# Queueing the early loads in the order of need and starting attention from q and k

## The chip, the cores and the metric

One core of one Trainium2 chip. Times are device microseconds of that core: each kernel is executed several times, and the median is quoted. Profiles are of one execution, whose span is some 2 us shorter than the quoted time. A run is called slow when it is over 1.5% above the fastest of its kernel; only fast runs are compared. Ratios below are the mean time of one kernel's fast runs over that of the other's of the same rounds on the same chip, so not quite the ratio of the medians quoted beside them.

## The reference, cut to what matters

```python
x: (1, 2048, 1024) bf16            # S = 2048, D = 1024, 32 heads of 32
# block A: pre-LN, local dilated attention: 8 keys per position, 2 apart
q, k, v = layernorm(x) @ wqkv
logits  = einsum(q, k[pos - 2*w]) * 32**-0.5     # w = 0..7, masked at the start
h       = x + (softmax(logits) @ v[...]) @ wo
# block B: pre-LN, bilinear GLU, F = 3584
h2      = h + ((layernorm(h) @ w_gate) * (layernorm(h) @ w_up)) @ w_down
```

## The kernel before

The sequence is cut into four chunks of 512 positions. TensorE runs the qkv projections of all chunks, then per chunk the output projection and the GLU. VectorE runs the local attention of each chunk beside that, on data that goes through DRAM to change its layout: the projection is evicted by ScalarE, stored (`qd`, `kd`, `vd`), loaded again (`qD`, `kD`, `vD`), and the attention output goes the same way back (`od`, `oT`). The attention and the layer norms of chunks 1 to 3 are Python generators. A counter (`bg.now`) advances by 1.73 for each group of eight matmuls emitted, and decides where in the program order the generators' instructions are put. Each engine executes its own instructions in that order (in the profile after, for one, ScalarE stands 21.58 us before one activation, and the evictions placed behind it wait as well).

The early part of it:

```python
    load_x0(0)                  # four row tiles of chunk 0, and
    load_x0(1)
    load_w(2)                   # ... projection block 0 (1 MB, two halves)
    load_x0(2)
    load_w(2)                   # ... projection block 1
    load_x0(3)
    ...
    def first_transpose(t):     # chunk 0: transposed by TensorE
        pts[t] = psum.tile([128, KO, 128], BF, tag="mm", name=f"pt{t}")
        for kk in range(KO):
            nc.tensor.transpose(pts[t][:, kk, :], lns[t][:, bass.ts(kk, 128)], ident[:])
        nc.scalar.copy(lnTs[0][:, 0:4, bass.ts(t, 128)], pts[t][:, 0:4, :])
    def first_copy(t):
        nc.vector.tensor_copy(lnTs[0][:, 4:8, bass.ts(t, 128)], pts[t][:, 4:8, :])
    ...
    nc.gpsimd.tensor_copy(order_after_x0[:], x0[3][:, 0:1])
    pump()                      # SyncE: blocks 2 to 5 and half of wo
    bg.add(ln1(1))              # these load their own rows, on GpSimd's queue;
    bg.add(ln1(2))              # each norm is followed by its DMA transpose on SyncE
```

and the order of the main part:

```python
    def start_attention(c):
        stored.add(c)
        atts[c] = attention(c)          # for c == 0: load q, k, v, then 7.0 later
        bg.add(atts[c], bg.now + (5.0 if c == 0 else 0.0))

    qkv(0, range(1, 6))
    bg.add(ln1(3))
    start_attention(0)
    qkv(1, range(6))
    start_attention(1)
    qkv(2, range(6))
    start_attention(2)
    ...
    qkv(3, range(4), last=True)
    bg.finish(atts[0])
    nxt = wo_ln2(0)                     # needs oT of chunk 0; VectorE adds and normalises
    qkv(3, range(4, 6), last=True)
    start_attention(3)
    for c in range(NCH):                # GLU, then the next chunk's output projection
        ...
```

Of the kernel before, what the change touches and what calls it, by code (L numbers as in the profile page):

```python
# [8 lines left out]
BF = mybir.dt.bfloat16  # L9
# [66 lines left out]
def kernel(  # L76
# [62 lines left out]
        for b in range(4):  # L139
            stream.append((("wd", NCH - 1, hf, b), wd_v[:, bass.ts(b, 7), bass.ts(hf, 512)], 7))  # L140
    wts = {}
    state = {"next": 0, "live": 0}

    def pump(eng=None):
        while state["next"] < len(stream) and state["live"] < 7:
            key, src, n = stream[state["next"]]
            wt = wpool.tile([128, KO, 512], BF, tag="w", name="w_" + "_".join(map(str, key)))
            (eng or nc.sync).dma_start(wt[:, 0:n, :], src)
            wts[key] = wt
            state["next"] += 1  # L150
            state["live"] += 1

# [20 lines left out]
    def ln_tiles(name):  # L173
        mv4 = small.tile([128, 4, nc.vector.BN_AGGR_DIM], F32, tag="mv4", name="mv" + name)
        rs4 = small.tile([128, 4], F32, tag="rs4", name="rs" + name)
        return mv4, rs4

    def load_x(c, what, eng):
        tiles = []
        for t in range(4):  # L180
            xt = hp.tile([128, D], BF, tag="h", name=f"{what}{c}_{t}")
            eng.dma_start(xt[:], x[bass.ds(c * TC + t * 128, 128), :])
            tiles.append(xt)
        return tiles

    lnTs = {}

    def ln1(c):
        xts = load_x(c, "x", nc.gpsimd)
        yield "later", 8.0 if c < 3 else 5.0  # L190
        lnTs[c] = lnTp.tile([128, KO, TC], BF, tag="lnT", name=f"lnT1_{c}")
        mv4, rs4 = ln_tiles(f"1_{c}")

        def norm(t):
            ln = normalize(xts[t], mv4, rs4, t)
            nc.sync.dma_start_transpose(lnTs[c][:, :, bass.ts(t, 128)], ln[:])

        for t in range(4):
            stats(xts[t], mv4, t)
            rstd_of(mv4, rs4, t, t + 1)  # L200
            yield 1.5
            if t > 0:
                norm(t - 1)
                yield 0.55
        norm(3)
        yield 0.55


    def load_w(parts=1):
        key, src, n = stream[state["next"]]  # L210
        wt = wpool.tile([128, KO, 512], BF, tag="w", name="w_" + "_".join(map(str, key)))
        for q in range(parts):
            nc.sync.dma_start(wt[:, bass.ts(q, KO // parts), :], src[:, bass.ts(q, KO // parts), :])  # L213
        wts[key] = wt
        state["next"] += 1
        state["live"] += 1

    x0 = [hp.tile([128, D], BF, tag="h", name=f"x0_{t}") for t in range(4)]

    def load_x0(t):  # L220
        nc.sync.dma_start(x0[t][:], x[bass.ds(t * 128, 128), :])  # L221

    load_x0(0)
    load_x0(1)
    load_w(2)
    load_x0(2)
    load_w(2)
    load_x0(3)
    nc.scalar.preload_act_table_set("natural_log_exp_and_others")
    warm = const.tile([128, 512], BF)  # L230
# [52 lines left out]
        lns[t] = normalize(x0[t], mv0, rs0, t)  # L283

    def first_transpose(t):
        pts[t] = psum.tile([128, KO, 128], BF, tag="mm", name=f"pt{t}")
        for kk in range(KO):
            nc.tensor.transpose(pts[t][:, kk, :], lns[t][:, bass.ts(kk, 128)], ident[:])  # L288
        nc.scalar.copy(lnTs[0][:, 0:4, bass.ts(t, 128)], pts[t][:, 0:4, :])  # L289

    def first_copy(t):
        nc.vector.tensor_copy(lnTs[0][:, 4:8, bass.ts(t, 128)], pts[t][:, 4:8, :])  # L292

    def first_mm(t, kos):
        for ko in kos:
# [20 lines left out]
        if t < 3:  # L316
            first_rstd(t + 1)
    first_mm(3, range(8))
    order_after_x0 = const.tile([128, 1], BF)
    nc.gpsimd.tensor_copy(order_after_x0[:], x0[3][:, 0:1])  # L320
    pump()
    bg.add(ln1(1))
    bg.add(ln1(2))
    for j in range(4):
# [35 lines left out]
    def prefetch_qk(c):  # L360
        if c in stored and ("q", c) not in qkv_in:
            load_qk(c)

    def attention(c):
        if c == 0:
            load_qk(0)
            load_v(0)
            yield "later", 7.0
        qD, kD, vD = qkv_in["q", c], qkv_in["k", c], qkv_in["v", c]
        lg = att.tile([128, W, SUB], F32, tag="lg", name=f"lg{c}")  # L370
        for wp in range(W // 2):
            prod = att.tile([128, 2, DH, SUB], BF, tag="prod", name=f"prod{c}_{wp}")
            for j in range(2):
                o = HB - DIL * (2 * wp + j)
                nc.vector.tensor_tensor(prod[:, j], qD[:], kD[:, :, o:o + SUB], ALU.mult)  # L375
                yield 2.3
            nc.vector.tensor_tensor(prod[:, :, 0:16], prod[:, :, 0:16], prod[:, :, 16:32], ALU.add)  # L377
            yield 2.3
            nc.vector.tensor_tensor(prod[:, :, 0:8], prod[:, :, 0:8], prod[:, :, 8:16], ALU.add)
            yield 1.2  # L380
            t3 = att.tile([128, 2, 4, SUB], F32, tag="t3", name=f"t3{c}_{wp}")
            nc.vector.tensor_tensor(t3[:], prod[:, :, 0:4], prod[:, :, 4:8], ALU.add)
            yield 1.2
            nc.vector.tensor_tensor(t3[:, :, 0:2], t3[:, :, 0:2], t3[:, :, 2:4], ALU.add)
            nc.vector.tensor_tensor(lg[:, 2 * wp:2 * wp + 2, :], t3[:, :, 0], t3[:, :, 1], ALU.add)
            yield 1.0
        if c == 0:
            nc.vector.tensor_tensor(lg[0:32, :, 0:16], lg[0:32, :, 0:16], mask[:], ALU.add)
        tr = att.tile([128, 4, SUB], F32, tag="t3", name=f"tr{c}")
        nc.vector.tensor_tensor(tr[:], lg[:, 0:4], lg[:, 4:8], ALU.max)  # L390
        nc.vector.tensor_tensor(tr[:, 0:2], tr[:, 0:2], tr[:, 2:4], ALU.max)
        mx = att.tile([128, SUB], F32, tag="mx", name=f"mx{c}")
        nc.vector.tensor_tensor(mx[:], tr[:, 0], tr[:, 1], ALU.max)
        nc.vector.tensor_tensor(lg[:], lg[:], mx[:, None, :].to_broadcast((128, W, SUB)), ALU.subtract)
        nc.scalar.activation(lg[:], lg[:], ACTF.Exp, scale=float(DH) ** -0.5)
        yield 3.5
        tr2 = att.tile([128, 4, SUB], F32, tag="t3", name=f"trs{c}")
        nc.vector.tensor_tensor(tr2[:], lg[:, 0:4], lg[:, 4:8], ALU.add)
        nc.vector.tensor_tensor(tr2[:, 0:2], tr2[:, 0:2], tr2[:, 2:4], ALU.add)
        sm = att.tile([128, SUB], F32, tag="mx", name=f"sm{c}")  # L400
        nc.vector.tensor_tensor(sm[:], tr2[:, 0], tr2[:, 1], ALU.add)
        rs = att.tile([128, SUB], F32, tag="rs", name=f"rs{c}")
        nc.vector.reciprocal(rs[:], sm[:])
        yield 2.5
        prefetch_qk(c + 1)
        at = att.tile([128, W, SUB], BF, tag="at", name=f"at{c}")
        nc.vector.tensor_tensor(at[:], lg[:], rs[:, None, :].to_broadcast((128, W, SUB)), ALU.mult)
        yield 1.2
        oD = att.tile([128, DH, SUB], BF, tag="oD", name=f"oD{c}")
        for wp in range(W // 2):  # L410
            pv = att.tile([128, 2, DH, SUB], BF, tag="prod", name=f"pv{c}_{wp}")
            for j in range(2):
                w = 2 * wp + j
                o = HB - DIL * w
                nc.vector.tensor_tensor(pv[:, j], vD[:, :, o:o + SUB],  # L415
                                        at[:, w, None, :].to_broadcast((128, DH, SUB)), ALU.mult)
                yield 2.3
            prefetch_qk(c + 1)
            if wp == 0:
                nc.vector.tensor_tensor(oD[:], pv[:, 0], pv[:, 1], ALU.add)  # L420
                yield 2.3
            else:
                nc.vector.tensor_tensor(pv[:, 0], pv[:, 0], pv[:, 1], ALU.add)  # L423
                yield 2.3
                nc.vector.tensor_tensor(oD[:], oD[:], pv[:, 0], ALU.add)  # L425
                yield 2.3
        nc.gpsimd.dma_start(od[c].rearrange("c g d s -> (c g) d s"), oD[:])
        oT = att.tile([128, KO, 4, SUB], BF, tag="oT", name=f"oT{c}")
        for cp in range(4):
            nc.gpsimd.dma_start(oT[:, :, cp, :], od[c][cp].rearrange("(hg hl) d s -> (hl d) hg s", hl=4))  # L430
        oTs[c] = oT
        while c + 1 < NCH and ("q", c + 1) not in qkv_in:
            yield "later", 1.0
            prefetch_qk(c + 1)
        if c + 1 < NCH:
            load_v(c + 1)
# [86 lines left out]
    def start_attention(c):  # L523
        stored.add(c)
        atts[c] = attention(c)
        bg.add(atts[c], bg.now + (5.0 if c == 0 else 0.0))

    qkv(0, range(1, 6))
    bg.add(ln1(3))
    start_attention(0)  # L530
    qkv(1, range(6))
    start_attention(1)
    qkv(2, range(6))
    start_attention(2)
    hss[0] = load_x(0, "h", nc.sync)
# [43 lines left out]
```

## Time and profile before

| | |
|---|---|
| time, median of 6 runs | 820.2 us (819.98 to 820.9) |
| span of the profiled run | 817.9 us, granted clock 1.000 |
| TensorE busy | 806.0 us (99%) |
| dense matmuls begin | 20.0 us |
| first attention product on VectorE (chunk 0) | 67.6 us |
| output projection of chunk 0 begins | 165.05 us |
| first gate matmul (chunk 0) | 192.7 us |

How a wait between engines is read: in a timeline, the bracket behind an instruction gives the time its engine sat idle just before it and what ended that. In the view of waits only waits of the named engine are counted. For this kernel TensorE has none after 18.2 us.

### The profile page before, as it was taken

What the parts mean: (1) busy time and instruction counts of PE and PEld (TensorE: products, weight loads), DVE (VectorE), ACT (ScalarE), POOL (GpSimd) and SP (SyncE); (2) the same over time, 40 slices, a digit from 0 to 9 for tenths busy, and PEclk for the clock granted to TensorE, in tenths of its full rate; (3) what the DMA queues carried; (4) which work ended last, traced back from release to release, by engine and by line L of the source; (5) the groups of instructions that cost most, each with busy time, mean ns of one, the idle gap of its engine ahead of it and who ended that gap; (6) DMA issues with size and microseconds to landing.
All of it is one profiled execution on the core that took longest, in us unless ns stands there. A gap on an engine that the chain in (4) does not pass through costs nothing.

```text
span 817.9 us, 9732 instructions
## 1 busy us (share of the span) xinstructions
PE 806.0 (99%) x3808; PEld 373.7 (46%) x3881; DVE 470.5 (58%) x520; ACT 222.4 (27%) x505; POOL 31.2 (4%) x60
## 2 busy tenths in 40 slices
PE   7999999999999999999999999999999999999998
PEld 5444444444444444444444444444444444444445
DVE  4539999998888899968887995111124111111011
ACT  2545444323333310023333000333320003333100
POOL 3100000200000200000200002000000000000000
PEclk9999999999999999999999999999999999999999
DMA  9999864999845969755863688636456753535400
GB/s 309 318 207 241 160 192 114 260 265 276 283 135 169 289 174 305 241 168 185 272 215 123 126 263 269 206 109 198 150 179 160 229 188 125 185 117 170 146 26 26
DMA packets 194494, 158.98 MB, mean 194 GB/s; under 512 B 83472, under 2 KB 188048, under 8 KB 192400
## 3 DMA queue, kind: packets, MB, share of 16 engines
q1 hardware_dynamic: 189904, 133.19, 57.4%
q0 software_dynamic: 4544, 25.17, 9.2%
q8 instruction: 30, 0.49, 0.3%
q14 instruction: 16, 0.13, 0.1%
HBM read 128.97 MB, written 22.02 MB: 185 GB/s over the span
## 4 chain that ended last, share of the span: by engine, by line
PE 97%; DMA 1%; issue 1%; SPq 0%; DVE 0%; ACT 0%
PE pg L330 24%; PE pu L330 24%; PE acc L512 21%; PE ps L330 19%; PE wo L453 7%; PE accl L502 3%; DMA x<-in_A_x_dram 1%; SPq L213 0%; PE ps L297 0%; SPq L221 0%; PE pt L288 0%; ACT lnT L289 0%; DVE ln L170 0%; DVE h L493 0%; DVE lnT L292 0%
## 5 line engine op out<-in xcount | busy, mean ns | idle before, releaser
L330 PE MATMUL pg<-lnT,w_wg 128*128 128x512 bf16 x879 | 210.1, 379 | 0.9
L330 PE MATMUL pu<-lnT,w_wu 128*128 128x512 bf16 x877 | 209.8, 379 | 0.9
L512 PE MATMUL acc<-w_wd,gs 128*128 128x512 bf16 x768 | 169.0, 379 | 0.8
L484 DVE TENSOR_TENSOR gs<-gs,us 128x512 bf16<-128x512 bf16 x112 | 47.4, 423 | 198.7 <-ACT us L483 198.7
L330 PE MATMUL ps<-lnT,w_qkv 128*128 128x512 bf16 x721 | 158.4, 379 | 0.8
L330 PEld LDWEIGHTS <-w_wg 128*128 128x128 bf16 x896 | 87.7, 98 | 105.7
L330 PEld LDWEIGHTS <-w_wu 128*128 128x128 bf16 x896 | 87.7, 98 | 105.7
L478 ACT CAST gs<-pg 128x512 bf16<-128x512 f32 x112 | 65.6, 586 | 235.9 <-PE pg L330 231.4
L512 PEld LDWEIGHTS <-gs 128*128 128x128 bf16 x784 | 76.7, 98 | 92.5
L330 PEld LDWEIGHTS <-w_qkv 128*128 128x128 bf16 x736 | 72.0, 98 | 86.6
L483 ACT CAST us<-pu 128x512 bf16<-128x512 f32 x112 | 65.6, 586 | 123.8 <-PE pu L330 114.6
L249 ACT CAST sg<-ps 128x512 bf16<-128x512 f32 x96 | 55.4, 586 | 63.8 <-PE ps L330 58.7
L415 DVE TENSOR_TENSOR pv<-vD,at 128x4096 bf16<-128x4096 bf16 x32 | 72.4, 2287 | 0.4
L375 DVE TENSOR_TENSOR prod<-qD,kD 128x4096 bf16<-128x4096 bf16 x32 | 72.3, 2285 | 0.1
L493 DVE TENSOR_TENSOR h<-acc,h 128x512 bf16<-128x512 f32 x28 | 17.4, 683 | 78.4 <-PE acc L512 78.4
L453 PE MATMUL wo<-w_wo,oT 128*128 128x512 bf16 x251 | 55.6, 379 | 0.3
L453 PEld LDWEIGHTS <-oT 128*128 128x128 bf16 x256 | 25.1, 98 | 30.2
L377 DVE TENSOR_TENSOR prod<-prod 128x4096 bf16<-128x4096 bf16 x16 | 36.6, 2289 | 0.3
L165 ACT ACTIVATE rs<-mv,eps 128x1 f32<-128x1 f32 x32 | 9.4, 294 | 75.7 <-DVE mv L162 70.8
L423 DVE TENSOR_TENSOR pv<-pv 128x4096 bf16<-128x4096 bf16 x12 | 27.5, 2289 | 0.2
L425 DVE TENSOR_TENSOR oD<-oD,pv 128x4096 bf16<-128x4096 bf16 x12 | 27.4, 2287 | 0.2
L502 PE MATMUL accl<-w_wd,gs 128*128 128x512 bf16 (+1 forms) x139 | 24.4, 336 | 0.1
(56 smaller groups left out, 291.3 us busy)
## 6 DMA issues: line engine op xcount, KB each, us to landing
w_wg<-in_B_w_gate_dram SPq DMA_DIRECT2D x28, 1024.0 KB, 7.0
w_wu<-in_B_w_up_dram SPq DMA_DIRECT2D x28, 1024.0 KB, 5.4
w_wd<-in_B_w_down_dram SPq DMA_DIRECT2D x32, 896.0 KB, 6.2
w_wo<-in_A_wo_dram SPq DMA_DIRECT2D x8, 1024.0 KB, 6.8
kd<-sg SPq DMA_DIRECT2D x32, 144.0 KB, 3.0
vd<-sg SPq DMA_DIRECT2D x32, 144.0 KB, 3.7
kD<-kd POOLq DMA_DIRECT2D x4, 1152.0 KB, 7.7
vD<-vd POOLq DMA_DIRECT2D x4, 1152.0 KB, 11.1
```

The lines of the kernel that those rows point to most:

```text
L249: nc.scalar.copy(sg[:, HB:HB + TC], ps[:])
L330: nc.tensor.matmul(ps[:], lhsT=wt[:, ko, bass.ts(j, 128)], rhs=rhs[:, ko, :], start=(ko == 0), stop=(ko == KO - 1))
L375: nc.vector.tensor_tensor(prod[:, j], qD[:], kD[:, :, o:o + SUB], ALU.mult)
L377: nc.vector.tensor_tensor(prod[:, :, 0:16], prod[:, :, 0:16], prod[:, :, 16:32], ALU.add)
L415: nc.vector.tensor_tensor(pv[:, j], vD[:, :, o:o + SUB], at[:, w, None, :].to_broadcast((128, DH, SUB)), ALU.mult)
L423: nc.vector.tensor_tensor(pv[:, 0], pv[:, 0], pv[:, 1], ALU.add)
L453: nc.tensor.matmul(ps[:], lhsT=oTs[c][:, kk, t, :], rhs=wts["wo", c, hf][:, kk, :], start=(kk == 0), stop=(kk == KO - 1))
L478: nc.scalar.copy(gs[:], pg[:])
L483: nc.scalar.copy(us[:], pu[:])
L484: nc.vector.tensor_tensor(gs[:], gs[:], us[:], ALU.mult)
L502: nc.tensor.matmul(acc[:], lhsT=hT[f][:, bass.ts(t, 128)], rhs=wts["wd", c, hf, f // 7][:, f % 7, bass.ds(lo, n)], start=(f == 0), stop=(f ...
L512: nc.tensor.matmul(acc[t][:], lhsT=hT[f][:, bass.ts(t, 128)], rhs=wts["wd", c, hf, b][:, j, :], start=(f == 0), stop=(f == NF - 1))
```

## The change

The intent: load things in the order in which they are needed, so that chunk 0's rows are not behind a weight block that comes later; give all early loads to one queue; and begin the attention of chunk 0 as soon as q and k are there, without waiting for v.

```diff
-    load_w(2)
+    load_w0(0, 4)                 # block 0, first half
     load_x0(2)
-    load_w(2)
+    load_w0(4, 4)                 # block 0, second half
     load_x0(3)
 ...
-        pts[t] = psum.tile([128, KO, 128], ...)          # one PSUM tile, two readers
+        for hf in range(2):
+            pt = psum.tile([128, KO // 2, 128], ...)     # one for each reader
 ...
-    nc.gpsimd.tensor_copy(order_after_x0[:], x0[3][:, 0:1])
-    pump()
+    w1 = wpool.tile([128, KO, 512], BF, tag="w", name="w_qkv_1")
+    nc.gpsimd.tensor_copy(w1[:, 0, 0:1], x0[3][:, 0:1])   # block 1 waits for x's tile 3
+    pump(2, w1)
+    xtiles[1] = load_x(1, "x", nc.sync)
+    pump(3)
+    xtiles[2] = load_x(2, "x", nc.sync)
+    pump(6)
     bg.add(ln1(1))
     bg.add(ln1(2))
 ...
-    qkv(0, range(1, 6))
+    qkv(0, range(1, 4))
     bg.add(ln1(3))                # its four transposes wait until block 5 is emitted
+    load_qk(0)
     start_attention(0)            # bg.now + 12.0 instead of 5.0 + 7.0
+    qkv(0, range(4, 6))
+    emitted.add("qkv0")
+    load_v(0)
     qkv(1, range(6))
     start_attention(1)
+    pump(len(stream))             # wo is loaded from here
```

(Cut: the `limit` of `pump`, chunk 3's rows on SyncE, and the wait of attention for v just before its softmax is applied.)

More of the change, by code (lines that the diff above doesn't have):

```diff
@@ L141, with pump @@
     wts = {}
-    state = {"next": 0, "live": 0}
-    def pump(eng=None):
-        while state["next"] < len(stream) and state["live"] < 7:
+    state = {"next": 0, "live": 0, "limit": 1}
+    def pump(limit=None, wt=None):
+        state["limit"] = limit or state["limit"]
+        while state["next"] < state["limit"] and state["live"] < 7:
             key, src, n = stream[state["next"]]
-            wt = wpool.tile([128, KO, 512], BF, tag="w", name="w_" + "_".join(map(str, key)))
-            (eng or nc.sync).dma_start(wt[:, 0:n, :], src)
+            if wt is None:
+                wt = wpool.tile([128, KO, 512], BF, tag="w", name="w_" + "_".join(map(str, key)))
+            nc.sync.dma_start(wt[:, 0:n, :], src)
             wts[key] = wt
+            wt = None
             state["next"] += 1
@@ L186, with transpose @@
     lnTs = {}
+    xtiles = {}
+    emitted = set()
     def ln1(c):
-        xts = load_x(c, "x", nc.gpsimd)
-        yield "later", 8.0 if c < 3 else 5.0
-        lnTs[c] = lnTp.tile([128, KO, TC], BF, tag="lnT", name=f"lnT1_{c}")
+        if c == 2:
+            xtiles[3] = load_x(3, "x", nc.sync)
+        xts = xtiles[c]
         mv4, rs4 = ln_tiles(f"1_{c}")
+        lns = [None] * 4
+        def transpose(t):
+            if c not in lnTs:
+                lnTs[c] = lnTp.tile([128, KO, TC], BF, tag="lnT", name=f"lnT1_{c}")
+            nc.sync.dma_start_transpose(lnTs[c][:, :, bass.ts(t, 128)], lns[t][:])
         def norm(t):
-            ln = normalize(xts[t], mv4, rs4, t)
-            nc.sync.dma_start_transpose(lnTs[c][:, :, bass.ts(t, 128)], ln[:])
+            lns[t] = normalize(xts[t], mv4, rs4, t)
+            if c < 3:
+                transpose(t)
         for t in range(4):
@@ L206, in ln1, with load_w0 @@
         yield 0.55
-    def load_w(parts=1):
-        key, src, n = stream[state["next"]]
-        wt = wpool.tile([128, KO, 512], BF, tag="w", name="w_" + "_".join(map(str, key)))
-        for q in range(parts):
-            nc.sync.dma_start(wt[:, bass.ts(q, KO // parts), :], src[:, bass.ts(q, KO // parts), :])
-        wts[key] = wt
-        state["next"] += 1
-        state["live"] += 1
+        if c == 3:
+            while "qkv0" not in emitted:
+                yield "later", 1.0
+            for t in range(4):
+                transpose(t)
     x0 = [hp.tile([128, D], BF, tag="h", name=f"x0_{t}") for t in range(4)]
+    w0 = wpool.tile([128, KO, 512], BF, tag="w", name="w_qkv_0")
+    wts["qkv", 0] = w0
+    state["next"] += 1
+    state["live"] += 1
     def load_x0(t):
         nc.sync.dma_start(x0[t][:], x[bass.ds(t * 128, 128), :])
+    def load_w0(lo, n):
+        nc.sync.dma_start(w0[:, lo:lo + n, :], wqkv_v[:, lo:lo + n, 0:512])
     load_x0(0)
     load_x0(1)
-    load_w(2)
+    load_w0(0, 4)
     load_x0(2)
-    load_w(2)
+    load_w0(4, 4)
     load_x0(3)
@@ L285, in first_transpose @@
     def first_transpose(t):
-        pts[t] = psum.tile([128, KO, 128], BF, tag="mm", name=f"pt{t}")
-        for kk in range(KO):
-            nc.tensor.transpose(pts[t][:, kk, :], lns[t][:, bass.ts(kk, 128)], ident[:])
-        nc.scalar.copy(lnTs[0][:, 0:4, bass.ts(t, 128)], pts[t][:, 0:4, :])
+        for hf in range(2):
+            pt = psum.tile([128, KO // 2, 128], BF, tag="mm", name=f"pt{t}_{hf}")
+            for kk in range(KO // 2):
+                nc.tensor.transpose(pt[:, kk, :], lns[t][:, bass.ts(4 * hf + kk, 128)], ident[:])
+            pts[t, hf] = pt
+        nc.scalar.copy(lnTs[0][:, 0:4, bass.ts(t, 128)], pts[t, 0][:])
     def first_copy(t):
-        nc.vector.tensor_copy(lnTs[0][:, 4:8, bass.ts(t, 128)], pts[t][:, 4:8, :])
+        nc.vector.tensor_copy(lnTs[0][:, 4:8, bass.ts(t, 128)], pts[t, 1][:])
     def first_mm(t, kos):
@@ L318 @@
     first_mm(3, range(8))
-    order_after_x0 = const.tile([128, 1], BF)
-    nc.gpsimd.tensor_copy(order_after_x0[:], x0[3][:, 0:1])
-    pump()
+    w1 = wpool.tile([128, KO, 512], BF, tag="w", name="w_qkv_1")
[5 more added lines that the diff above has]
+    pump(6)
     bg.add(ln1(1))
@@ L364, in attention @@
     def attention(c):
-        if c == 0:
-            load_qk(0)
-            load_v(0)
-            yield "later", 7.0
-        qD, kD, vD = qkv_in["q", c], qkv_in["k", c], qkv_in["v", c]
+        qD, kD = qkv_in["q", c], qkv_in["k", c]
         lg = att.tile([128, W, SUB], F32, tag="lg", name=f"lg{c}")
@@ L405, in attention @@
         prefetch_qk(c + 1)
+        while ("v", c) not in qkv_in:
+            yield "later", 1.0
+        vD = qkv_in["v", c]
         at = att.tile([128, W, SUB], BF, tag="at", name=f"at{c}")
@@ L525, in start_attention @@
         atts[c] = attention(c)
-        bg.add(atts[c], bg.now + (5.0 if c == 0 else 0.0))
-    qkv(0, range(1, 6))
+        bg.add(atts[c], bg.now + (12.0 if c == 0 else 0.0))
+    qkv(0, range(1, 4))
     bg.add(ln1(3))
+    load_qk(0)
     start_attention(0)
+    qkv(0, range(4, 6))
+    emitted.add("qkv0")
+    load_v(0)
     qkv(1, range(6))
     start_attention(1)
+    pump(len(stream))
     qkv(2, range(6))
```

## The prediction

Its sum came to 820.8 + 12.6, about 833 us. Passages on hardware behaviour that no trace showed at the time are cut, and each cut is marked. One term goes, in ScalarE's limit of (d): that limit came to 205.1 with the term, and is 192.7 - 2.4 + 13.1 = 203.4 without it. The sum rests on VectorE's limit, 205.3, and is unchanged. The eight banks, and the 49 = 41 + 8 groups in (d), come from the kernel's PSUM pool (`bufs=8`), one buffer for each group of eight matmuls. At the 8 matmuls in 1.73 us that the chain before shows, eight buffers are 13.8 us of TensorE's work (an estimate from these two numbers; in the changed kernel TensorE stopped 12.9 us after ScalarE's wait began). The 0.9 per transpose in the first rival is assumed, not measured; the estimate from packet times is 1.55.

> **What bounds the kernel now.** I read the page first (busy shares), then busy time by stretch, the chain of work, and last the timelines of ScalarE, GpSimd, SyncE and VectorE in the first 190 us.
>
> ```profile
> PE 806.0 (99%) x3808; PEld 373.7 (46%) x3881; DVE 470.5 (58%) x520; ACT 222.4 (27%) x505; POOL 31.2 (4%) x60
> 0.00:10.00 10.00, 7.37 (x45) 3.66 (x45) 4.97 (x12) 2.87 (x6) 1.43 (x15) 1.00 0.78 255
> 10.00:22.00 12.00, 9.92 (x137) 8.21 (x139) 6.21 (x15) 4.71 (x12) 4.79 (x9) 1.00 1.07 363
> 22.00:50.00 28.00, 27.89 (x129) 12.70 (x130) 11.49 (x25) 11.85 (x43) 2.71 (x5) 1.00 1.12 293
> ```
>
> TensorE is the bound: 12 us idle in 818. From 22 us on it is full (27.89 of 28; the rest is missing records), so only the start (and 3.4 us of tail, untouched) can be won. The start:
>
> ```profile
> 5.09 7.61 DMA x<-in_A_x_dram
> ...
> 15.19 0.42 DVE lnT L292
> ...
> 16.93 0.64 PE pt L288 x8
> 17.57 0.02 issue
> 17.59 0.59 ACT lnT L289
> 18.19 0.04 issue
> 18.23 1.95 PE ps L297 x32
> ```
>
> The fourth row tile of x lands at 12.70; normalise, transpose, copy and the last 32 small matmuls follow, and the dense stream starts at 20.0.
>
> The other thing to see is how little slack the dense stream has, in the timelines of ScalarE, GpSimd and VectorE (start, us, instruction; in brackets the idle time before it and what ended it):
>
> ```profile
> 46.70 0.29 ACT L165 ACTIVATE rs<-mv,eps 128x1 f32<-128x1 f32 x1 [5.62 <-DVE mv L162]
> ...
> 51.19 0.29 ACT L165 ACTIVATE rs<-mv,eps 128x1 f32<-128x1 f32 x1 [3.18 <-DVE mv L162]
> ...
> 112.61 1.06 ACT L395 ACTIVATE lg<-lg 128x1024 f32<-128x1024 f32 x1 [3.76 <-DVE lg L394]
> ```
>
> ```profile
> 58.28 0.54 POOL L352 DMA_DIRECT2D kD<-kd x1 [17.45 <-DMA kd<-sg]
> ```
>
> ```profile
> 67.61 4.49 DVE L375 TENSOR_TENSOR prod<-qD,kD 128x4096 bf16<-128x4096 bf16 x2
> ...
> 169.03 0.68 DVE L455 TENSOR_TENSOR h<-wo,h 128x512 bf16<-128x512 f32 x1
> ```
>
> ScalarE empties the projection's PSUM banks in order with the small rstd and softmax activations. When one of those waits for VectorE, evictions stop while TensorE fills the eight banks. Before, that never lasted long enough to stop TensorE. Attention of chunk 0 starts on VectorE at 67.61, because its k load is issued only at 58.28, after 17.45 us of waiting for the last k store.
>
> [...] The chain has 8 in 1.73 us, 216 each[...]. [...] 9 us of waits on ScalarE (46.70 and 51.19) cost TensorE nothing. [...] the DMA share is 1.07 and 1.12 from 10 to 50 us, whichever queue issues. [...]
>
> **The change part by part.**
>
> (a) Start. Before, both first weight blocks (2 MB) go ahead of x's fourth tile; now only block 0. That tile then has 2 MB in front of and including it instead of 3 MB. At the 359 GB/s measured between the third tile (9.05) and the fourth (12.70) it lands 2.9 us earlier, near 9.7. The transposes now write two PSUM tiles, and in the built program VectorE's copy waits for TensorE alone, not for ScalarE's copy. Per row tile the repeat was 3.0 us (normalise at 13.33 and 16.33) when data was there. After, it is TensorE: 8 transposes 0.46, 8 matmuls 0.61, 24 matmuls 1.5, 2.6 in all. The second half of block 0 now lands near 9.0, which sets the second tile's transposes to 9.5, the fourth's to 9.5 + 2 x 2.6 = 14.7, the last 32 matmuls to 15.8-17.75. The dense stream starts at 17.75, not 20.18: 2.4 us gained.
>
> (b) The early queue. Block 1 waits for x's fourth tile, a GpSimd copy (0.19) and 1.1 us to its first byte (the first load: issue 0.76, first packet 1.88): data from 11.2. Then come x1, block 2, x2, blocks 3 to 5, all ahead of the q stores in SyncE's queue. Each block is needed 6.9 us after the last and takes 2.9, so none is late.
>
> (c) Attention earlier. In the built program the first attention product stands where TensorE is near 50.5 us (block 3 ends at 38.5, plus the 12.0 of its delay); before, near 66.6, and VectorE got there at 67.6. So 16 us of program order are moved ahead. Does its k arrive 16 us earlier? I add the DMA work that must pass before the last k store, with costs per item from the trace between 12.7 and 58.2 us, when the DMA is saturated (packet times summed, over 16 engines, over an overlap of 1.12): 2.89 per MB of weights, 2.72 per MB of x rows, 2.46 for the q load, 0.78 per q store, 0.63 per k store, 1.55 per DMA transpose. The changed queue puts before that store: blocks 1 to 5 14.5, x1 to x3 8.2, q load 2.5, 8 q stores 6.2, 8 k stores 5.0, and now all eight transposes of chunks 1 and 2, 12.4 (before it was five). Sum 48.8 from 11.2: it lands near 60, against 58.2 before. The output weight's 2.9 us that left the queue is eaten by three more transposes (4.7) and 1.5 us of idle DMA at the block 1 wait. The k load then takes 8 to 9 us (9.3 before, issue to first product): VectorE starts at T = 68.8, 18 us behind its place.
>
> (d) What that costs. First, ScalarE: the softmax exponential stands after the eviction of TensorE's 41st dense group. VectorE needs 45.0 us from first product to it (67.6 to 112.6), then 1.06 + 0.6, so the next eviction ends at 68.8 + 46.7 = 115.5. TensorE has run out of banks at 17.75 + 49 x 1.727 = 102.4: 13.1 us of stall. (A smaller stop, some 2 to 3 us, at chunk 3's rstd, which waits through VectorE for chunk 2's transposes, falls inside it.) Second, VectorE: before, the first output-projection sum came 101.4 us after the first product. The changed order puts 18.5 us more attention ahead of it (rest of prod_1 3.6, prod_2 10.4, half of prod_3 4.5): 68.8 + 119.9 = 188.7. From there to the first gate matmul LN2 takes 13.3 (14.5 less the 1.2 that no longer lies between) and its last transpose 3.3: 205.3. Before, that matmul started at 192.7: +12.6 us. The two limits nearly coincide[...], and the larger holds; the 2.4 us of (a) is inside it and is lost. After it the VectorE order has slack again and the rest is unchanged.
>
> Sum: 820.8 + 12.6, about 833.
>
> **The rivals.** One: k lands early (near 43), attention starts in its place, and only (a) shows: 818.4. For it: the author's 12.0 looks tuned, and the old 5 + 7 matched its trace to 1 us. Against it: even at 350 GB/s for all and 0.9 per transpose the work of (c) ends past 50, T past 58, and T above 56 already stops TensorE. Two: the last k store lands still later (transposes alone on the queue moved only 36 GB/s for 2 us around 56): each us of T is one us of time; T = 73 gives 837.6, over the 2% line of 837.2. Three: a weight block or rows late in the dense stream: block 2 is due at 24.6, lands near 20.7; 4 us of slack, so unlikely. Four: the delay is absorbed because attention ends late anyway; against it, VectorE reaches the first output sum at 169.03, 2 us after TensorE's group, so there is no slack to absorb it.
>
> **Range and chances.** The time is T + 764.6, T = 68.8 with some 4 us either way for the DMA sum (10% of 48.8) and the k load (1 us): 828 to 838. One chance in ten for much less stall widens the low side: 824 to 839. Slower by over 2% needs T above 72.6: 0.16. Faster by over 2% (804.4) is impossible with TensorE busy 806: 0.01.
>
> **What would show it.** Dense stream from near 17.75 (a); DMA busy without a gap from 11.2 to 60 and the k load issued near 60 (c); ScalarE idle some 25 us before chunk 0's exponential near 114, with TensorE waiting for ScalarE there some 13 us[...], and the first gate matmul near 205 (d). A k load issued before 50, or a full TensorE from 90 to 120, would make the prediction wrong.

## More of the kernel before

The page gives busy tenths in 40 slices; TensorE and its granted clock before:

```profile
PE   7999999999999999999999999999999999999998
PEclk9999999999999999999999999999999999999999
```

The kernel is bound by TensorE from the second slice to the last. A change can gain only at the two ends, or lose in the middle.

## The result, and the profile after

| | before | after |
|---|---|---|
| time, median of 6 runs | 820.2 us | 833.62 us (832.6 to 834.67) |
| ratio | | 1.0163 (1.015 to 1.0176) |
| granted clock, mean | 1.000 | 0.991 |
| dense matmuls begin | 20.0 | 16.94 us |
| k load of chunk 0 issued | 58.28 | 61.53 us |
| first attention product | 67.61 | 69.57 us |
| first gate matmul | 192.7 | 206.65 us |

The slices after:

```profile
PE   8989949999999999999999999999999999999998
PEclk9999979999999999999999999999999999999999
```

The start is shorter, and there are two new holes: a small one in slice 3, and a large one in slice 6, where the clock falls as well. TensorE's waits, and the group of the dense projection matmuls (count, busy us, mean ns, then idle before and what ended it):

```profile
engine line waited for: us in total, times, longest us
PE ps L352 <- ACT halo L273: 12.9, 2, 10.6
```

```profile
L352 PE MATMUL ps<-lnT,w_qkv 128*128 128x512 bf16 x721 | 162.4, 385 | 13.9 <-ACT halo L273 12.9 <-issue 0.2
```

Before, the same group had 158.4 us busy and 0.8 idle. The same matmuls are 4.0 us longer, and TensorE waits 12.9 us for ScalarE to free PSUM banks. The timelines of TensorE, ScalarE, GpSimd and VectorE after show from the end backwards why:

```profile
55.69 6.59 PE L352 MATMUL ps<-lnT,w_qkv 128*128 128x512 bf16 x22 [2.32 <-ACT halo L273]
...
116.47 4.00 PE L352 MATMUL ps<-lnT,w_qkv 128*128 128x512 bf16 x9 [10.58 <-ACT halo L273]
```

```profile
54.33 0.29 ACT L168 ACTIVATE rs<-mv,eps 128x1 f32<-128x1 f32 x1 [3.30 <-DVE mv L165]
...
114.58 1.06 ACT L413 ACTIVATE lg<-lg 128x1024 f32<-128x1024 f32 x1 [21.58 <-DVE lg L412]
```

```profile
61.53 0.55 POOL L374 DMA_DIRECT2D kD<-kd  x1 [20.60 <-DMA vd<-sg]
```

```profile
69.57 4.50 DVE L393 TENSOR_TENSOR prod<-qD,kD 128x4096 bf16<-128x4096 bf16 x2 [9.09 <-DMA kD<-kd]
...
189.54 1.28 DVE L476 TENSOR_TENSOR h<-wo,h 128x512 bf16<-128x512 f32 x2
```

TensorE stops at 105.9 because ScalarE, between two evictions, waits 21.58 us for the logits from which the softmax exponential is made. VectorE had sat idle for 9.09 us until k landed, and began 2 us later than before, though its place in the program order is 16 us earlier. (The k load waits on several semaphores. The profile names the last, a v store, but what it needs are the k stores.) The smaller stop, from 53.4, has the same form: ScalarE waits 3.30 us, until 54.33, for the statistics of which chunk 3's rstd is made (the reciprocal of the standard deviation in its layer norm; late_both, below, shows that it is this one). Then the clock. Busy time by stretch in the two holes; the last columns are the granted clock, the DMA share and GB/s:

```profile
57.00:58.00 1.00, 1.00 (x4) 0.32 (x3) 0.00 (x0) 0.97 (x5) 0.00 (x0) 0.50 1.00 227
...
118.00:120.00 2.00, 2.00 (x6) 0.76 (x5) 1.93 (x3) 2.00 (x6) 0.00 (x0) 0.50 0.75 170
```

TensorE counts as busy there, but at a granted clock of 0.50: 6 matmuls are listed in the 2 us from 118 to 120, where 2 us at 1.00 list 10 or 11 (122 to 124: 11; a matmul at an edge counts on both sides). The clock was 0.50 from 55.95 to 59.36 and from 110.56 to 120.80, and 1.00 just before and after each. What brings this on is not shown: here a stop of 2.32 us (53.37 to 55.69) was followed by it, while in late_att2 one of 2.33 us (53.87 to 56.20) was not (1.00 from 50 to 70). The account, up to the first gate matmul: start 3.1 us earlier, stops 12.9 + 0.2, matmuls at the lower clock 4.0: -3.1 + 13.1 + 4.0 = +14.0. Measured: 206.65 - 192.68 = 13.97. After it, the two kernels run alike.

### The profile page after: what moved, and what is told of

It is laid out like the page before. It is cut to its first block, busy times and chain, and to the rows that moved or that the text cites. A ratio compares the mean times of both kernels' runs of the same rounds, so it can differ in the third digit from the quotient of the medians.

```text
span 831.7 us, 9716 instructions
## 1 busy us (share of the span) xinstructions
PE 809.1 (97%) x3808; PEld 374.5 (45%) x3881; DVE 471.3 (57%) x520; ACT 220.8 (27%) x505; POOL 24.6 (3%) x48
## 4 chain that ended last, share of the span: by engine, by line
PE 88%; DVE 6%; DMA 4%; issue 1%; SPq 1%; ACT 0%; DVEq 0%
PE pg L352 23%; PE pu L352 23%; PE acc L533 20%; PE ps L352 11%; PE wo L474 7%; PE accl L523 3%; DVE prod L393 2%; DMA lnT<-ln 1%; DVE prod L395 1%; DMA kD<-kd 1%; PE ps L315 1%; DMA w_qkv<-in_A_wqkv_dram 1%; DVE t L400 1%; DVE prod L397 1%; DVE st L164 1%
## 5 line engine op out<-in xcount | busy, mean ns | idle before, releaser
L352 PE MATMUL ps<-lnT,w_qkv 128*128 128x512 bf16 x721 | 162.4, 385 | 13.9 <-ACT halo L273 12.9
```

The source lines that it names most:

```text
L352: nc.tensor.matmul(ps[:], lhsT=wt[:, ko, bass.ts(j, 128)], rhs=rhs[:, ko, :], start=(ko == 0), stop=(ko == KO - 1))
```

## The experiments

Ten runs of nine kernels, all correct. In the first set of rounds (early_only, start_only, late_att, late_both) one profiled run (late_att) fell in the slow state at a granted clock of 0.753 (1067.74 us), and one run of the kernel before at 0.949 (853.0 us). They are left out of the ratios and of the medians below. A ratio whose interval includes 1 (start_only, late_att, late_both, old_start) does not show a difference from the kernel before. The two single runs have no interval: they serve for their traces only.

| run | ratio to before (95%) | median us | before us | first product | first gate matmul |
|---|---|---|---|---|---|
| early_only | 1.0107 (1.0065 to 1.0149) | 829.52 | 820.34 | 66.68 | 201.81 |
| start_only | 1.0035 (0.9986 to 1.0083) | 825.31 | 820.34 | 68.59 | 198.74 |
| late_att | 1.0036 (0.9982 to 1.0089) | 825.42 | 820.34 | - | - |
| late_att2 (same kernel) | 1.0066 (1.0049 to 1.0084) | 825.93 | 820.19 | 69.77 | 199.23 |
| late_both | 1.0023 (0.9987 to 1.006) | 823.14 | 820.34 | 68.45 | 196.17 |
| k_first | 1.0073 (1.0059 to 1.0087) | 825.92 | 820.19 | 62.59 | 199.31 |
| k_first_d22 | 0.996 (0.9947 to 0.9972) | 816.62 | 820.19 | 63.47 | 189.70 |
| old_start | 1.0003 (0.9987 to 1.002) | 819.75 | 819.67 | 65.18 | 192.15 |
| queue_only | one run | 824.55 | 820.19 | 69.09 | 197.98 |
| psum_only | one run | 818.85 | 819.67 | 66.77 | 191.84 |

### Is it the program order, or the load queue?

**early_only**: the kernel before, its queue and start untouched, with only the order changed.

```diff
-    qkv(0, range(1, 6))
-    bg.add(ln1(3))
-    start_attention(0)            # bg.now + 5.0, then 7.0
+    qkv(0, range(1, 4))
+    x3 = load_x(3, "x", nc.gpsimd)
+    bg.add(ln1(3))                # transposes after block 5
+    load_qk(0)
+    start_attention(0)            # bg.now + 12.0
+    qkv(0, range(4, 6))
+    load_v(0)
```

> The kernel before, with its own load queue and start, and only chunk 3's layer norm and the attention of chunk 0 moved ahead in program order as in the change. Theory: k arrives as before (first product 67 to 69), the exponential stands 9 groups earlier, TensorE stops for 8 us or more there: 828 to 833. Rival (queue is the cause): 819 to 822.

829.52 us. VectorE and TensorE in its timelines:

```profile
66.68 4.50 DVE L387 TENSOR_TENSOR prod<-qD,kD 128x4096 bf16<-128x4096 bf16 x2
```

```profile
113.58 60.75 PE L346 MATMUL ps<-lnT,w_qkv 128*128 128x512 bf16 x272 [6.95 <-ACT halo L273]
```

k came about when it always came, and the stop is there with the old queue. The earlier place in the order, by itself, makes most of the loss (a ratio of 1.0107, where the whole change has 1.0163). In the changed kernel the first product also comes 2.9 us later than here. By the prediction's own sum this kernel, with 16.3 instead of 18.5 us of attention ahead of the first sum (117.76 us after the first product in this trace, 101.42 before), should take T + 762.4 = 829.1 us. Both limits of (d) in the prediction move one for one with the first product, so this sum does not tell which of them holds; the waits do. After the start TensorE waits for ScalarE alone, and that stop ends 46.9 us after the first product here (66.68 and 113.58) and in the changed kernel (69.57 and 116.47), and 46.8 us after it in k_first (62.59 and 109.42). The prediction had 46.7.

**late_att**: the changed kernel with the attention's place put back (28.0 instead of 12.0 after block 3, which puts the exponential and the first sum of the output projection where they were before).

> The changed kernel with one number changed: attention of chunk 0 begins 28 instead of 12 after block 3, which puts the exponential and the first output-projection sum exactly where they stand in the kernel before. Theory (program order ahead of the k load): the 10.6 us stop before the exponential goes, first product still near 69.6, and 820 to 822 remains, because chunk 3's early rstd still stops TensorE by some 2 us near 55 and the start still gains 3.2. Rival (the new load queue itself slows the kernel): it stays within 3 us of 833.6.

Fast runs 821.06, 825.42 and 826.26. It was run again:

> The kernel of late_att again, since its profile fell in the slow state. Expected as its fast runs: 821 to 826, with TensorE waiting for the attention output near 165 and for ScalarE near 55.

825.93 us, and not the 820 to 822 first expected. The stop before the exponential is gone, as it should be, but a new one stands at the output projection:

```profile
169.16 16.41 PE L474 MATMUL wo<-w_wo,oT 128*128 128x512 bf16 x63 [3.89 <-DMA oT<-od]
```

So my account was incomplete. Even with the order restored, the gain of the start did not come through. TensorE was ready for the attention output at 165.27 (169.16 less the wait), no earlier than before: the expected stop near 55 (2.33 us) had used up the gain. And the output was later than before: its loads were issued at 162.43 instead of 158.20.

**late_both**: as late_att, and chunk 3's layer norm after block 5 again (attention 15.0 after block 5, the same place).

```diff
-    qkv(0, range(1, 4))
+    qkv(0, range(1, 6))
+    emitted.add("qkv0")
     bg.add(ln1(3))
     load_qk(0)
-    start_attention(0)            # + 12.0
-    qkv(0, range(4, 6))
-    emitted.add("qkv0")
     load_v(0)
+    start_attention(0)            # + 15.0
```

> As the run before, and chunk 3's layer norm begins after block 5 again, as in the kernel before; loads and start as in the changed kernel. Theory: no stop of TensorE after 17 us, the start's 3.2 us come through whole: 816.5 to 818. Rival (new load queue harms): above 825.

823.14 us. TensorE has no stop near 55 any more (so the small one was indeed chunk 3's rstd), but waits 4.1 us for the attention output: it was ready at 162.74, 2.3 us earlier than before, and the output's loads were issued at 160.20, 2.0 us later. The expectation failed in the same way.

### Where the gain of the start goes

**start_only**: the kernel before with the new first loads and the split PSUM tile, and nothing else.

```diff
     load_x0(1)
-    load_w(2)
+    load_w0(0, 4)
     load_x0(2)
-    load_w(2)
+    load_w0(4, 4)
     load_x0(3)
 ... (two PSUM tiles per transpose, block 1 behind x's tile 3, as in the change)
```

> The kernel before with only block 0 ahead of x's fourth tile (block 1 behind it) and the two PSUM tiles per transpose. Both theories: dense stream from 17 instead of 20, kept to the end: 816.5 to 818. If the start's gain is swallowed later by itself: 819.5 to 821.

The dense stream began at 17.19 instead of 20.0, but neither expected time came: the fastest of the four runs took 821.73 us, the median 825.31. (The interval of the ratio includes 1. That the gain is gone is shown; that the kernel became slower is not.) GpSimd, SyncE and TensorE around the first output projection, before:

```profile
152.11 0.54 POOL L427 DMA_DIRECT2D od<-oD  x1 [46.70 <-DVE oD L425]
152.52 0.44 SPq L148 DMA_DIRECT2D w_wg<-in_B_w_gate_dram  x1
158.20 3.55 POOL L430 DMA_DIRECT2D oT<-od  x4 [5.54 <-DMA od<-oD]
165.05 13.98 PE L453 MATMUL wo<-w_wo,oT 128*128 128x512 bf16 x63
```

and in start_only:

```profile
152.06 0.44 SPq L148 DMA_DIRECT2D w_wg<-in_B_w_gate_dram  x1
153.10 0.54 POOL L441 DMA_DIRECT2D od<-oD  x1 [46.70 <-DVE oD L439]
161.94 3.54 POOL L444 DMA_DIRECT2D oT<-od  x4 [8.29 <-DMA od<-oD]
168.45 16.63 PE L467 MATMUL wo<-w_wo,oT 128*128 128x512 bf16 x64 [3.71 <-DMA oT<-od]
```

Before, the first of the `oT` loads was issued at 158.20 and took 6.2 us to land, near 164.4 (an estimate from these two numbers), and TensorE wanted it at 165.05. There were 0.65 us to spare, and this is what the prediction did not see: the attention chain of chunk 0, from the k load over 84 us of VectorE and two trips through DRAM, was timed to TensorE within a microsecond.

In start_only TensorE was ready at 164.74 (168.45 less its wait), only 0.3 us earlier than before: most of the 2.8 us had already gone in two small stops (0.46 us for a weight block at 24.7, 1.55 us for ScalarE at 54.1). It is the attention output that came later, by 4 us. The first product came 1.0 us later (68.59), and from the issue of the store `od` to the loads that wait for it took 8.8 us instead of 6.1. The wait then costs more than its own length, since the 64 matmuls behind it take 16.63 us where they took 13.98 (the granted clock is 0.50 from 168 to 172).

Why the store takes longer was not tested, but the traces have a pattern. In the seven kernels in which the store was issued ahead of SyncE's 1 MB load of the first gate block (`w_wg`), as before, it took 5.4 to 6.9 us from its issue to that of the loads that wait for it; in the four in which it was issued 1.0 to 2.9 us behind that load (start_only, queue_only, late_att2, late_both) 7.2 to 8.8. So a k that is 1 us late may push the store behind the weight load. It is not that TensorE is ahead: in k_first_d22, below, TensorE is 3.0 us ahead and the store takes 5.4.

**queue_only** and **psum_only**: the two halves of that start, one look each.

> The kernel before with only block 0 ahead of x's fourth tile, one PSUM tile per transpose as before: one look for the start. Dense stream from 18.5 to 19.5 if the serial copies of the two engines matter (3.0 us per tile), 17 if the load order alone gives the 3 us.

Dense stream from 18.67, as expected for the serial copies; 824.55 us, with a wait of 4.0 us for the attention output. Its first product came 1.5 us later than before (69.09): in this run, as in start_only, the new order of the loads goes with a later k.

> The kernel before with only the two PSUM tiles per transpose: one look for the start. The third and fourth tile of x still land at 9.0 and 12.7, so only the copies behind the fourth get shorter: dense stream 0.5 to 1.2 us before 20.0.

Dense stream from 19.17, as expected. 818.85 us in one run, without a wait for the attention output. The 0.8 us did not use up the slack, since here the attention output came earlier as well (first product at 66.77, its loads issued at 157.58 instead of 158.20). Separately the two move the dense start by 1.3 and 0.8 us, together by 2.8. A likely reason, not tested, is that with the fourth tile of x there sooner the shorter copies pay in every tile.

### What sets the arrival of k

**k_first**: the changed kernel, with chunk 2's four transposes behind the k stores in SyncE's queue. Chunks 2 and 3 normalise in place so that no layer-norm buffer is waited for.

```diff
-            lns[t] = normalize(xts[t], mv4, rs4, t)
-            if c < 3:
+            if c < 2:
+                lns[t] = normalize(xts[t], mv4, rs4, t)
+            else:                               # in place
+                lns[t] = xts[t]
+                nc.vector.tensor_scalar(xts[t][:], xts[t][:], mv4[:, t, 0:1], rs4[:, t:t + 1], ...)
+            if c < 2:
                 transpose(t)
 ...
-        if c == 3:
-            while "qkv0" not in emitted:
+        if c >= 2:
+            while ("k0" if c == 2 else "qkv0") not in emitted:
                 yield "later", 1.0
             for t in range(4):
                 transpose(t)
 ...
     qkv(0, range(1, 4))
+    emitted.add("k0")
```

> The changed kernel with chunk 2's four DMA transposes put behind the eight k stores in SyncE's queue (chunks 2 and 3 normalise in place, so that nothing waits for a layer-norm buffer); the place of attention in program order is that of the change. Theory (what stands ahead of the last k store sets the first product, each us of it is one us of time): k load issued near 55 instead of 61.5, first product near 63 instead of 69.6, time 825 to 829. Rival (the k load waits for its stores whatever stands between): first product above 68, 833.

825.92 us. GpSimd, VectorE and TensorE:

```profile
56.24 0.55 POOL L378 DMA_DIRECT2D kD<-kd  x1 [14.72 <-DMA kd<-sg]
```

```profile
62.59 4.50 DVE L397 TENSOR_TENSOR prod<-qD,kD 128x4096 bf16<-128x4096 bf16 x2 [6.51 <-DMA kD<-kd]
```

```profile
109.42 62.42 PE L356 MATMUL ps<-lnT,w_qkv 128*128 128x512 bf16 x274 [6.32 <-ACT halo L277]
```

With the program order of the change, and only four transposes out of the way and two chunks normalised in place, the k load is issued 5.3 us sooner, the first product comes 7.0 us sooner, TensorE's longest wait shrinks from 10.58 to 6.32, and the time falls by 7.7 us (in different sets of rounds: 833.62 and 825.92, with kernels before of 820.2 and 820.19). The prediction's T + 764.6 gives 827.2 here. One rival is not separated: the run takes away not only the DMA work of these transposes, but also the time that SyncE waited for VectorE before issuing transposes (7.4 us up to 62 us in the changed kernel, 1.8 us here). The k stores behind them wait too: in the changed kernel a transpose holds SyncE for 4.51 us from 45.50, and the next k store is issued at 50.10.

**k_first_d22**: the same, with attention placed where k now arrives.

```diff
-    bg.add(ln1(3))
+    bg.add(ln1(3), bg.now + 6.0)
 ...
-        bg.add(atts[c], bg.now + (12.0 if c == 0 else 0.0))
+        bg.add(atts[c], bg.now + (22.0 if c == 0 else 0.0))
```

> As k_first, with attention 22 instead of 12 after block 3 and chunk 3's layer norm 6 us later, so that program order matches the arrival of k. Theory (a shorter start pays only if the attention output is also ready earlier at the first output projection): no wait of TensorE for it near 162, the start's 3 us kept: 816.5 to 818.5. Rival (the output's arrival doesn't depend on k): TensorE waits near 162 again, 821 to 825.

816.62 us (816.51 to 817.1), faster than the kernel before by 0.4% (its slowest run is faster than the fastest of the kernel before, 819.26), and than the changed kernel by 17 us. TensorE does not wait once after the start:

```profile
162.08 13.98 PE L478 MATMUL wo<-w_wo,oT 128*128 128x512 bf16 x63
```

The attention output was asked for at 153.32 (158.20 before). With 6.2 us to land it was there near 159.5 (an estimate), 2.6 us before TensorE wanted it at 162.08. The stop near 55 is gone too, which fits the later start of chunk 3's layer norm (as in late_both).

**old_start**: k_first_d22 with the start of the kernel before.

> k_first_d22 with the start of the kernel before put back: both weight blocks ahead of x's fourth tile, one PSUM tile per transpose; everything else as in k_first_d22. Theory (the earlier k gains nothing by itself, it only lets the shorter start through): 819.5 to 820.8, the time of the kernel before. Rival (the earlier k or the normalising in place is itself worth some us): 816 to 818.

819.75 us, against 819.67 for the kernel before: the earlier k gains nothing alone. Neither of the two is shown to gain anything without the other; together they are worth 3.6 us.

## Why the prediction was right or wrong

The time, 833.0, was met (833.62), by the mechanism that it named. By its own steps:

- **(a) Start.** Right in kind, too small: 3.1 us instead of 2.4. The mis-sized term is the repeat per row tile: the transposes of tiles 1 to 3 stand at 9.31, 11.70 and 14.10, 2.40 apart, not 2.6, since the 8 and the 24 small matmuls run through in 2.11 without a pause. That this gain is lost was right, and held more widely than was said: without any change of program order it is lost too (start_only), for another reason than the prediction's, the later attention output.
- **(b) Early queue.** Right: no wait of TensorE for a weight block in the dense stream.
- **(c) Arrival of k.** The sum of DMA work put the last k store near 60; the load that waits for it was issued at 61.53. The costs per item, summed from packet times before the change (12.7 to 58.2 us): 0.78 us per 128 KB in 256-byte pieces (one mean over q stores and transposes), 0.63 per 144 KB store in 288-byte pieces, against 2.89 per MB of weights in 1 KB pieces. The first product was predicted at 68.8 and came at 69.57. k_first moved four of the counted items and the product moved by 7.0 us (the sum says 4 x 1.55 = 6.2), though it also removed waits of SyncE (see there).
- **(d) ScalarE's limit.** Right, but cut differently: 13.1 us predicted for one stop that hides the smaller, 10.58 + 2.32 measured in two. The term cut from this limit (205.1 less 203.4) stood for a lower clock after one stop and was too small: the granted clock was 0.50 after both, and the same matmuls took 4.0 us longer. The prediction said that the smaller stop falls inside the larger: their sum was indeed unchanged, but the lower clock after the smaller one (0.50 from 55.95 to 59.36) was left out.
- **(d) VectorE's limit.** The first sum of the output projection came 119.97 us after the first product (119.9 predicted). But the prediction let this limit set the end, and it did not: TensorE has no wait for chunk 0's second layer norm. It came to the first gate matmul at 206.65 on its own, 17.1 us after that sum, where 16.6 was allowed. The ScalarE path, 1.5 us longer than predicted (205.1, with the cut term), was the bound. "The larger holds" was right; the larger was the other one. That the total was met all the same is partly luck: the two limits lie within 0.5 us of each other (189.54 + 16.6 = 206.1 and 206.65).
- **Rivals.** One (k arrives early) is refuted by the k load at 61.53. Two by the same number. Three by TensorE's waits. Four had the right ground and the wrong extent: "no slack to absorb it" is a statement on VectorE after the output projection, while the attention output itself had 0.65 us to spare. In late_att2, late_both and start_only it came later by more than that.

What stays open: whether the gate block's load is what makes the attention output's store longer (6.1 and 8.8 us), how much of k's delay is DMA work and how much SyncE's waiting in order, and why single runs of the kernel before take 825 to 826 us at a mean clock of 0.997 to 0.998. With 0.65 us to spare, a late attention output would look like that, but no such run was profiled.

## What to carry to other kernels

When instructions of a background stage are placed by a model of time, moving the placement ahead does not move the data (here 16 us of placement, and a first product 2.0 us later): first add up what stands in the DMA queue before the transfer that starts the stage. An instruction placed before its data holds up what stands behind it: here ScalarE stood 21.58 us before the exponential, and TensorE, which in this kernel has eight PSUM buffers to fill, stopped at 105.9, 12.9 us after ScalarE's wait began. A stage that ends just in time is a constraint even if no wait shows in the profile: before shortening what runs beside it, compare when its result lands with when it is wanted, ask whether the change delays that result, and shorten both.
